# In-place closing operations, half-width tiles at the end, and a second output queue, in a gated mix of local attention and a token MLP

## The chip, the cores and the metric

The kernel runs on one core of one Trainium2 chip. The core has five engines with a queue each: TensorE multiplies matrices into PSUM (eight banks, each of 512 fp32 values in each of 128 partitions), VectorE and ScalarE do elementwise work, GpSimd does little here, and SyncE (SP) issues transfers. Transfers are issued from SP's or ScalarE's queue and run on 16 DMA engines. Engines wait for each other through semaphores. The metric is the device time of one execution in microseconds (us), lower is better.

## What is computed

The output is a mix of two branches with a gate for each of 2048 positions:

```python
# x: [1, 2048, 512] bf16; 32 heads of 16; a window of 8 positions, each 2 apart
g = sigmoid((A_x * gate_w).sum(-1, keepdims=True))
a = local_attention(A_x @ A_wqkv) @ A_wo      # softmax over the window's 8 logits
h = layernorm(B_x)                            # over the 512 columns
u = gelu(einsum("bsd,sf->bdf", h, B_w1) + B_b1)     # mixes positions, F = 1792
b = (einsum("bdf,fs->bds", u, B_w2) + B_b2) transposed back to [1, 2048, 512]
out = g * a + (1 - g) * b
```

The kernel takes `A_x` for both branches, since the reference passes the same array to both (`x = A_x`).

## The kernel before, in words

The 2048 positions are cut into 16 tiles of 128 (`NST = 16`). The program runs in five stages that overlap across engines.

1. **Projections** (lines 626 to 670): Q, K and V come out transposed, columns in partitions, in groups of four matmuls (L631). The first groups are cut into 384 and 128 columns, so that matmuls of three widths occur.
2. **Attention weights** (674 to 781): VectorE multiplies Q and shifted K (L678), TensorE sums over a head's 16 columns (L686), VectorE and ScalarE make the softmax. Thirty-two transfers from ScalarE's queue spread the weights over partitions (L780, recorded as L436, the helper that makes every plain transfer).
3. **Weighted values** (783 to 795): VectorE multiplies V by the weights (L789) and adds the eight window positions, partly in place (L792), into `OT`, the attention's output before its last projection.
4. **MLP** (797 to 904): `ph2` multiplies the normalised x by B_w1 (L804), gelu follows on ScalarE, then `ph3` multiplies by B_w2 (L844), one accumulation of 14 matmuls for each of the 16 output tiles. ScalarE takes each tile out of PSUM with L898: T1[i] = (1 - g) * (y + b2), in bf16. `T1` lies where `X` was.
5. **Closing** (849 to 877, `emit_wo`): for each tile i, four matmuls of 512 columns (`wo_i`, L861) project OT with wo into one of the four PSUM banks 4 to 7, `WB(i)` = 4 + i mod 4. VectorE's closing operation (`cmb_i`, L873) computes g * PSUM + T1[i] and writes it into one of the four buffers `OUTS[i % 4]`. A transfer of 128 KB (`d_out_i`) takes that buffer to the output by SP's queue.

What waits for what is declared by names that an operation reads and writes: `cmb_i` reads the bank and `t1_i` and writes `outs(i % 4)`, which `d_out_i` reads. So `cmb_(i+4)` waits until `d_out_i` has landed, and `wo_(i+4)` until `cmb_i` has read its bank.

The order on each engine comes from a list planner (`_Sched.schedule`, 124 to 232). It repeatedly takes the operation that can start first by the planned durations, and breaks ties by the planned time that is left to the end behind it. Hand-written chains (923 to 937) fix VectorE's whole order, most of ScalarE's and a piece of TensorE's: `ph3b_14`, `wo_0` to `wo_3`, `ph3a_15`, `ph3b_15`, `wo_4`. So wo_4 to wo_15 are the last work on TensorE. At the end SP waits for the four semaphores of the output transfers (L981 to 984), and the program ends.

Of the kernel before, what the change touches and what calls it, by code (L numbers as in the profile page):

```python
# [5 lines left out]
BF16 = mybir.dt.bfloat16  # L6
FP32 = mybir.dt.float32
U8 = mybir.dt.uint8
ALU = mybir.AluOpType
# [4 lines left out]
D = 512  # L14
# [4 lines left out]
NST = S // 128  # L19
# [7 lines left out]
BURST_DELAY = 0.05  # L27
OUTQ = "sp"
XS = 384


class _Op:
# [302 lines left out]
def bass_gated_mix__sliding_local_dilated__mixer_token_mlp__prompt_kernel(nc, A_x, A_wqkv, A_wo, B_x, B_w1, B_b1, B_w2, B_b2, gate_w, out, dbg=None):  # L335
    with contextlib.ExitStack() as es:
        block = es.enter_context(nc.Block())
        view, pview, off, total = _views(nc, es)
        ps = es.enter_context(nc.psum_tensor("ps", [128, 8, 512], FP32))
        esem = {e: es.enter_context(nc.semaphore("sem_" + e)) for e in ("pool", "act", "dve", "pe")}  # L340
        sch = _Sched()
# [6 lines left out]
        outv = out[0].rearrange("(t p) d -> p t d", p=128)  # L348
# [13 lines left out]
        WO = view("WO", BF16, [(D, 4), (1, D)])  # L362
# [4 lines left out]
        OT = view("PBUF", BF16, [(S, 4), (1, S)])  # L367
        ATX = view("ATX", BF16, [(NW * HC, 8), (HC, NW), (1, HC)])
        ATT = view("ATT", BF16, [(NW * HC, 2), (HC, NW), (1, HC)])
        T1 = view("X", BF16, [(D, NST), (1, D)])  # L370
        OUTS = view("OUTS", BF16, [(D, 4), (1, D)])
        IDENT = view("IDENT", BF16, [(1, 128)])
        ONES = view("ONES", BF16, [(1, 128)])
        RP = view("RP", BF16, [(1, 32)])
# [23 lines left out]
        G = small(NST)  # L398
# [9 lines left out]
        def col(v_, i):  # L408
            return bass.AP(v_.tensor, v_.offset + i, [list(v_.ap[0]), [1, 1]])
# [11 lines left out]
        A = sch.add  # L421
# [13 lines left out]
        def mk_dma(dst, src):  # L435
            return lambda e: e.dma_start(dst, src)  # L436
# [42 lines left out]
        wq01 = ld_w(0, 0, 2, "act")  # L479
        ld_xt0(0, XS)  # L480
        xt0b = ld_xt0(XS, 512)
        wq23 = ld_w(0, 2, 2, "act")
# [16 lines left out]
        def ld_w1(j):  # L499
# [4 lines left out]
            if j < 4:  # L504
# [8 lines left out]
                       writes=["wo"], deps=throttle(), after=prev_dma(), name="d_wo")  # L513
# [4 lines left out]
        for i_, (v_, n_) in enumerate(((B_b1, NFT), (B_b2, NST), (gate_w, 4))):  # L518
            vr = v_.rearrange("(t q j) -> q t j", q=4, j=32)
            for q_ in range(4):  # L520
                sch.dma("sp", mk_dma(psub(BR, 32 * q_, n_, 32 * i_, [(1, 32)]), vr[q_]), n_ * 64, ds_b, reads=["br"],
                        writes=["br_%d_%d" % (i_, q_)], deps=throttle(), after=prev_dma(), name="d_b_%d_%d" % (i_, q_), issue=0.45)
        d_w1.append(ld_w1(3))
        A("dve", lambda e: e.transpose(out=BT, in_=BR), 0.2, reads=["br_%d_%d" % (i_, q_) for i_ in range(3) for q_ in range(4)],
          writes=["gwc"], name="t_b")
# [29 lines left out]
        for hf in range(2):  # L555
            t0 = 8 * hf
            for t in range(t0, t0 + 8):
                A("dve", (lambda t_: (lambda e: e.bn_stats(out=ST6[:, t_, :], in_=X[:, t_, :])))(t), 0.59,  # L558
                  reads=["x%d" % t], writes=["st6_%d" % t], name="ln1_%d" % t, prio=0)
# [7 lines left out]
                                                                    in1=cols(ZC, t0_, 8), op0=ALU.mult, op1=ALU.mult)))(t0),  # L567
# [5 lines left out]
              reads=["zc%d" % hf], writes=["sd%d" % hf], name="ln_sqrt%d" % hf, prio=0)  # L573
            A("dve", (lambda t0_: (lambda e: e.reciprocal(out=cols(RSTD, t0_, 8), in_=cols(SD, t0_, 8))))(t0), 0.25,
              reads=["sd%d" % hf], writes=["rstd%d" % hf], name="ln_rstd%d" % hf, prio=0)
            A("dve", (lambda t0_: (lambda e: e.scalar_tensor_tensor(
                out=cols(NMR, t0_, 8), in0=mv(t0_, 0), scalar=-0.5, in1=cols(RSTD, t0_, 8),
                op0=ALU.mult, op1=ALU.mult)))(t0),
# [68 lines left out]
        for (b0, d0, d1, s0, s1) in ((0, 0, 2, 0, XS), (0, 0, 2, XS, 512), (0, 2, 4, 0, 512), (4, 0, 4, 0, 512)):  # L647
            for b in range(b0, b0 + 4):
                tn, dl = first[b]
                last_main[0] = A("pe", f_proj(tn, dl, 0, b, d0, d1, s0, s1), 0.216 * (d1 - d0) * (s1 - s0) / 512,  # L650
                                 reads=ALLXT[s0 // 128:s1 // 128] + ["wqkv%d_%d" % (tn, dt) for dt in range(d0, d1)],
                                 writes=fbn[b], after=[last_main[0]], name="pf_%s%d_%d_%d" % (tnames[tn], dl, d0, s0))
        for b, (tn, dl) in enumerate(first):
            A("act", f_evq(tn, dl, 0, b), 0.52, reads=fbn[b] + (["k5pad"] if tn == 1 else []),
              writes=["%s5_%d_0" % (tnames[tn], dl)], name="ev_%s%d_0" % (tnames[tn], dl), prio=0)
# [7 lines left out]
        for (tn, dl, sb) in seq_proj:  # L663
            xr = ALLXT[4 * sb:4 * sb + 4]
            bank = main_bank()
            last_main[0] = A("pe", f_proj(tn, dl, sb, bank), 0.866,
                             reads=xr + ["wqkv%d_%d" % (tn, dt) for dt in range(4)],
                             writes=["acc%d" % bank], after=[last_main[0]], name="pj_%s%d_%d" % (tnames[tn], dl, sb), prio=0)
            A("act", f_evq(tn, dl, sb, bank), 0.62, reads=["acc%d" % bank] + (["k5pad"] if tn == 1 else ["v5pad"] if tn == 2 else []),
              writes=["%s5_%d_%d" % (tnames[tn], dl, sb)], name="ev_%s%d_%d" % (tnames[tn], dl, sb), prio=0)  # L670
# [26 lines left out]
        for wh in range(2):  # L697
# [6 lines left out]
            for (dl, c0, nc_) in pieces:  # L704
# [3 lines left out]
                  reads=["q5_%d_%d" % (dl, sb) for sb in range(c0, c0 + nc_)] +  # L708
                        ["k5_%d_%d" % (dl, sb) for sb in range(max(c0 - 1, 0), c0 + nc_)] + ["k5pad"],
                  writes=wr, name="qkm_%d_%d_%d" % (wh, dl, c0), prio=0)  # L710
                if c0 + nc_ == 4 and dl % 2 == 1:
# [4 lines left out]
                    else:  # L716
                        for wl in range(4):
                            qop = A("pe", f_qkr(prs, (wl,)), 0.5, reads=rd, writes=["lg%d_0" % (4 + wl), "lg%d_1" % (4 + wl)],
                                    name="qkr_%d_%d_%d" % (wh, dl, wl), prio=-100 + wl, delay=BURST_DELAY)
                            A("act", (lambda wh_, wl_: (lambda e: e.activation(out=ATT[:, :, 4 * wh_ + wl_, :], in_=ps[:, 4 + wl_, :].rearrange("p (h c) -> p h c", h=2), func=AF.Copy)))(wh, wl),  # L720
                              0.55, reads=["lg%d_0" % (4 + wl), "lg%d_1" % (4 + wl)], writes=["lw%d" % (4 * wh + wl)],
                              name="lev_%d_%d" % (wh, wl), prio=0)
# [18 lines left out]
        for hf in range(2):  # L741
            on = ["outs%d" % (2 * hf), "outs%d" % (2 * hf + 1)]
# [4 lines left out]
        for hf in range(2):  # L747
# [3 lines left out]
              reads=["outs1"], writes=["lh%d" % hf] + (wall if hf == 0 else []), name="sm_sub%d" % hf, prio=0)  # L751
            if hf == 0:
                A("act", lambda e: e.activation(out=col(SD, 0), in_=col(ZC, 0), func=AF.Exp, scale=0.0), 1.5,
                  reads=["zc0"], writes=["sd0"], name="sm_pre")
            A("act", (lambda hf_, l_: (lambda e: e.activation(out=ATT[:, hf_], in_=l_, func=AF.Exp)))(hf, lgh), 1.95,  # L755
              reads=["lh%d" % hf], writes=["att%d" % hf], name="sm_exp%d" % hf, prio=0)
        for hf in range(2):
# [5 lines left out]
            def f_rcp(e, hf_=hf):  # L763
# [6 lines left out]
              reads=["rs%d" % hf], writes=["att%d" % hf], name="sm_nrm%d" % hf, prio=0)  # L770
# [4 lines left out]
        for u in range(8):  # L775
            c, hf = u // 2, u % 2
            ds_at = sch.dsem("atx%d" % u)
            for a_ in range(4):
                dst = bass.AP(ATX.tensor, ATX.offset + a_ * pst + u * NW * HC, [[4 * pst, 32], [1, NW * HC]])
                sch.dma("act", mk_dma(dst, psub(ATT, 32 * c, 32, hf * NW * HC, [(1, NW * HC)])), 32 * NW * HC * 2, ds_at, issue=0.62,  # L780
                        reads=["att%d" % hf], writes=["atx_%d_%d" % (u, a_)], deps=pb_readers, name="d_atx_%d_%d" % (u, a_))
        USEQ = [0, 2, 1, 3, 4, 6, 5, 7]
        for k_, u in enumerate(USEQ):
            b_ = HC * u
            pv = PV[k_ % 2]
            pn = "pv%d" % (k_ % 2)
            in0 = sub(V5, PAD + b_, [(-2, NW), (KROW, 4), (1, HC)])
            in1 = sub(ATX, u * NW * HC, [(HC, NW), (0, 4), (1, HC)])
            A("dve", (lambda o_, i0, i1: (lambda e: e.tensor_tensor(out=o_, in0=i0, in1=i1, op=ALU.mult)))(pv, in0, in1), 4.4,  # L789
              reads=v_res + ["atx_%d_%d" % (u, a_) for a_ in range(4)], writes=[pn] + [qk_res, k_all][k_ % 2], name="avm_%d" % u)  # L790
            for (nm, n_, du) in (("ava", 4, 2.25), ("avb", 2, 1.2)):
                A("dve", (lambda pv_, n__: (lambda e: e.tensor_tensor(out=pv_[:, 0:n__], in0=pv_[:, 0:n__], in1=pv_[:, n__:2 * n__], op=ALU.add)))(pv, n_),  # L792
                  du, writes=[pn], name="%s_%d" % (nm, u))
# [15 lines left out]
        for ft in range(NFT):  # L809
            j = ft // 2  # L810
            bank = main_bank()
            for qt in range(4):
                last_main[0] = A("pe", f_ph2(ft, bank, qt), 0.864, reads=["x%d" % t for t in range(4 * qt, 4 * qt + 4)] + ["w1s%d" % (j % 4)],
                                 writes=["acc%d" % bank], after=[last_main[0]], name="ph2_%d_%d" % (ft, qt), prio=0)
            A("act", (lambda ft_, bank_: (lambda e: e.activation(out=UT[:, ft_, :], in_=ps[:, bank_, :], func=AF.Gelu_apprx_tanh,  # L815
                                                                bias=col(B1C, ft_))))(ft, bank), 0.72,
              reads=["acc%d" % bank, "b1c"], writes=["ut%d" % ft] + ALLXT,
              name="gel_%d" % ft, prio=0)
# [32 lines left out]
        def WB(i):  # L851
            return WOB[i % len(WOB)]

        def WBN(i):
            return ["lg%d_0" % WB(i), "lg%d_1" % WB(i)]

        def f_wo(i):
            def fn(e):
                ins = None
                for t in range(4):  # L860
                    ins = e.matmul(ps[:, WB(i), :], lhsT=OT[:, t, 128 * i:128 * i + 128], rhs=WO[:, t, :],  # L861
                                   start=(t == 0), stop=(t == 3))
                return ins
            return fn

        ds_out = [sch.dsem("out%d" % k) for k in range(4)]
        LAG = 4
        pending_wo = []

        def emit_wo(i):  # L870
            A("pe", f_wo(i), 0.866, reads=["ot%d" % (i // 2), "wo"], writes=WBN(i),
              name="wo_%d" % i, prio=0)
            A("dve", (lambda i_: (lambda e: e.scalar_tensor_tensor(out=OUTS[:, i_ % 4, :], in0=ps[:, WB(i_), :], scalar=col(G, i_),  # L873
                                                                   in1=T1[:, i_, :], op0=ALU.mult, op1=ALU.add)))(i), 0.75,
              reads=WBN(i) + ["g", "t1_%d" % i], writes=["outs%d" % (i % 4)], name="cmb_%d" % i, prio=0)
            sch.dma(OUTQ, mk_dma(outv[:, i, :], OUTS[:, i % 4, :]), 128 * D * 2, ds_out[i % 4], issue=(1.0 if OUTQ == "pool" else 0.5),
                    reads=["outs%d" % (i % 4)], name="d_out%d" % i)

        p3bank = {}

# [8 lines left out]
        for i in range(NST):  # L889
# [4 lines left out]
            elif i > 1:  # L894
                emit_ph3(i, 0)
            emit_ph3(i, 1)
            bank = p3bank[i]
            A("act", (lambda i_, bank_: (lambda e: e.activation(out=T1[:, i_, :], in_=ps[:, bank_, :], func=AF.Identity,  # L898
                                                               scale=col(OMG, i_), bias=col(C2, i_))))(i, bank), 0.8,
              reads=["acc%d" % bank, "omg", "c2"], writes=["t1_%d" % i, "x%d" % i],  # L900
              name="t1_%d" % i, prio=0)
# [18 lines left out]
        def lnr(hf):  # L920
# [5 lines left out]
              + ["ln3_%d" % t for t in range(NST) if t not in ln3_act] + ["qkm_1_2_0", "msk_0", "sm_ma0", "sm_mb0", "qkm_1_3_0",  # L926
                 "msk_1", "sm_ma1", "sm_mb1", "sm_m1", "sm_sub0", "sm_sub1", "g_omg", "g_c2", "g_g"]
              + ["%s%d" % (n_, h_) for h_ in range(2) for n_ in ("sm_sa", "sm_sb", "sm_s1", "sm_rcp", "sm_nrm")]
              + ["%s_%d" % (n_, u) for k_ in range(4) for n_ in ("avm", "ava", "avb", "avc") for u in USEQ[2 * k_:2 * k_ + 2]] + ["cmb_%d" % i for i in range(NST)])
        byname["d_w1_6"].deps.add(byname["d_atx_2_3"])  # L930
        chain(["d_w2_0", "d_th0", "d_w2_1", "d_th1", "d_w1_4", "d_w2_2", "d_w1_5", "d_w1_6"])
        def atn(u):
# [25 lines left out]
        def emit_engine(eng_name, e):  # L958
            for op in sch.order[eng_name]:
                for d in op.waits:  # L960
                    if d.is_dma:
                        e.wait_ge(d.dsem.handle, 16 * d.seq)
                    else:
                        e.wait_ge(esem[d.eng], d.seq)
                r = op.fn(e)
                if dbg is not None:
                    rr = r[-1] if isinstance(r, list) else r
                    dbg.setdefault("opmap", []).append((eng_name, op.name, rr.ins.name, op.start, op.end))
                if op.is_dma:
                    r.then_inc(op.dsem.handle, 16)  # L970
                elif op.sig:
                    if isinstance(r, list):
                        r = r[-1]
                    r.then_inc(esem[eng_name], 1)
            if eng_name == "sp" and dbg is not None and "keep" in dbg:
                for d in sch.dsems:
                    n_ = len([o for o in sch.ops if o.is_dma and o.dsem is d])
                    if n_ and d.queue == "sp":
                        e.wait_ge(d.handle, 16 * n_)
            if eng_name == OUTQ:  # L980
                for d in ds_out:  # L981
                    n_ = len([o for o in sch.ops if o.is_dma and o.dsem is d])
                    if n_:
                        e.wait_ge(d.handle, 16 * n_)

        @block.sync
        def _(e):
            emit_engine("sp", e)
# [44 lines left out]
```

## Time and profile before

| what | us |
|---|---|
| median of 3 runs (lowest to highest) | 171.76 (171.66 to 172.13) |
| the profiled execution's own time | 170.96 |
| span of that execution, first to last instruction | 169.2 |
| TensorE busy in the span (850 matmuls) | 163.5 |
| VectorE busy (122 instructions) | 142.8 |
| ScalarE busy (112 instructions) | 74.4 |
| closing operations, L873, 16 of 128 x 512 | 11.7 in all, mean 749 ns |
| output projection, L861, 62 recorded matmuls of 512 columns | 14.0 in all, mean 379 ns |
| output transfers, 16 of 128 KB, SP's queue | 1.7 median from issue to landing |
| mean granted TensorE clock | 0.998 of full speed |

A row "L861 PE MATMUL" is a group of instructions of that source line on that engine. "Busy" is the sum of their durations. Matmuls are pipelined: one is 379 ns long, and the next starts before it has ended, so the distance between starts tells what one costs in a stream. A number in square brackets is the idle time of the engine ahead of an instruction, with what ended it. "SPq" and "ACTq" are the queues in which SyncE and ScalarE issue transfers.

### The profile page before, as it was taken

The page shows a single profiled execution, that of the slowest core. Times are in us where ns is not written, and L with a number is a line of the kernel's source. Part 1 is how long each engine was busy: PE and PEld are TensorE (multiplying, and loading weights), DVE is VectorE, ACT ScalarE, POOL GpSimd, SP SyncE. Part 2 cuts the span into 40 slices and gives each one's busy share as a digit, 9 for nine tenths or more (in the row PEclk, how much of TensorE's full clock was granted, in tenths as well). Part 3 has the DMA queues.
Part 4 walks back from the last instruction along what each step waited for, and adds up shares of the span by engine and source line. Part 5 has one row for each costly group of instructions (what it writes and reads, how often), then busy time and mean ns, then how long its engine had stood idle before and what let it go on. Part 6 is the DMA issues. An engine that isn't in the chain of part 4 may idle for free.

```text
span 169.2 us, 2130 instructions
## 1 busy us (share of the span) xinstructions
PE 163.5 (97%) x850; PEld 76.5 (45%) x865; DVE 142.8 (84%) x122; ACT 74.4 (44%) x112; POOL 1.0 (1%) x9
## 2 busy tenths in 40 slices
PE   7999999999999999999999999999999999999992
PEld 2555555544444444444444444444444444444440
DVE  1009999999999963899999999999999999952874
ACT  0476698898979718691222131131221312211000
POOL 2000000000000000000000000000000000000000
PEclk9999999999999999999999999999999999999999
DMA  5999999939000989973789606472573470002234
GB/s 137 282 299 244 278 326 282 288 105 251 1 0 12 257 175 239 286 188 86 196 222 316 161 16 144 108 200 71 162 217 107 114 217 0 0 27 97 93 128 155
DMA packets 47313, 27.43 MB, mean 162 GB/s; under 512 B 11844, under 2 KB 46148, under 8 KB 47304
## 3 DMA queue, kind: packets, MB, share of 16 engines
q1 hardware_dynamic: 44696, 22.05, 48.6%
q10 hardware_dynamic: 2608, 5.25, 11.9%
q8 instruction: 7, 0.11, 0.3%
q14 instruction: 2, 0.02, 0.0%
HBM read 18.89 MB, written 2.11 MB: 124 GB/s over the span
## 4 chain that ended last, share of the span: by engine, by line
PE 93%; DMA 3%; ACT 2%; issue 1%; DVE 0%
PE ps L844 28%; PE ps L804 28%; PE ps L631 24%; PE ps L861 8%; PE ps L686 3%; DMA arena<-in_A_x_dram 3%; ACT arena L582 1%; DVE arena L873 0%; ACT arena L642 0%
## 5 line engine op out<-in xcount | busy, mean ns | idle before, releaser
L844 PE MATMUL ps<-arena 128*128 128x512 bf16 x220 | 48.5, 379 | 0.2
L804 PE MATMUL ps<-arena 128*128 128x512 bf16 x219 | 48.1, 379 | 0.5 <-ACT arena L582 0.2
L631 PE MATMUL ps<-arena 128*128 128x512 bf16 (+2 forms) x196 | 41.4, 370 | 0.7 <-issue 0.3
L678 DVE TENSOR_TENSOR arena<-arena 128x4096 bf16<-128x4096 bf16 (+1 forms) x12 | 35.6, 2991 | 0.0
L789 DVE TENSOR_TENSOR arena<-arena 128x8192 bf16<-128x8192 bf16 x8 | 35.0, 4419 | 0.0
L804 PEld LDWEIGHTS ps<-arena 128*128 128x128 bf16 x224 | 21.7, 98 | 26.8 <-issue 0.8
L844 PEld LDWEIGHTS ps<-arena 128*128 128x128 bf16 x224 | 21.9, 98 | 26.4
L631 PEld LDWEIGHTS ps<-arena 128*128 128x128 bf16 x200 | 21.9, 113 | 20.5 <-issue 1.0
L898 ACT ACTIVATE arena<-ps,arena 128x512 bf16<-128x512 f32 x16 | 12.5, 778 | 39.4 <-PE ps L844 35.6
L792 DVE TENSOR_TENSOR arena<-arena 128x4096 bf16<-128x4096 bf16 (+1 forms) x16 | 27.0, 1751 | 0.0
L642 ACT ACTIVATE arena<-ps 128x512 bf16<-128x512 f32 x32 | 18.9, 596 | 5.4 <-PE ps L631 5.2
L815 ACT ACTIVATE arena<-ps,arena 128x512 bf16<-128x512 f32 x14 | 9.6, 688 | 24.9 <-PE ps L804 24.7
L558 DVE BATCH_NORM_STATS2 arena<-arena 128x6 f32<-128x512 bf16 x16 | 10.1, 680 | 10.8 <-DMA arena<-in_A_x_dram 10.8
L873 DVE SCALAR_TENSOR_TENSOR arena<-ps,arena 128x512 bf16<-128x512 f32 x16 | 11.7, 749 | 6.7 <-PE ps L861 4.8
L861 PE MATMUL ps<-arena 128*128 128x512 bf16 x62 | 14.0, 379 | 0.1
L639 ACT ACTIVATE arena<-ps 128x512 bf16<-128x512 f32 x16 | 9.0, 596 | 3.8 <-PE ps L631 3.8
L861 PEld LDWEIGHTS ps<-arena 128*128 128x128 bf16 x64 | 6.3, 98 | 7.5
L582 ACT ACTIVATE arena<-arena 128x512 bf16<-128x512 bf16 x12 | 9.2, 803 | 0.0
L736 DVE TENSOR_TENSOR arena<-arena 128x512 bf16<-128x512 bf16 (+4 forms) x11 | 7.3, 667 | 0.8 <-ACT arena L755 0.5
L686 PE MATMUL ps<-arena 128*32 128x512 bf16 x128 | 7.6, 380 | 0.0
L794 DVE TENSOR_TENSOR arena<-arena 128x1024 bf16<-128x1024 bf16 x8 | 5.5, 688 | 0.1
L720 ACT ACTIVATE arena<-ps 128x512 bf16<-128x512 f32 x8 | 4.1, 603 | 2.5 <-PE ps L686 2.5
(42 smaller groups left out, 37.3 us busy)
## 6 DMA issues: line engine op xcount, KB each, us to landing
arena<-in_B_w_dram SPq DMA_DIRECT2D x7, 1024.0 KB, 7.9
arena<-in_B_w_dram SPq DMA_DIRECT2D x8, 896.0 KB, 5.2
arena<-arena ACTq DMA_DIRECT2D x32, 128.0 KB, 2.7
arena<-in_A_x_dram SPq DMA_DIRECT2D x4, 512.0 KB, 5.1
out_dram<-arena SPq DMA_DIRECT2D x16, 128.0 KB, 1.7
arena<-in_A_wqkv_dram ACTq DMA_DIRECT2D x2, 256.0 KB, 2.9
arena<-in_A_wqkv_dram ACTq DMA_DIRECT2D x1, 512.0 KB, 4.3
arena<-in_A_wqkv_dram SPq DMA_DIRECT2D x1, 512.0 KB, 7.1
```

Source lines behind the costliest of these rows:

```text
L582: A("act", (lambda t_: (lambda e: e.activation(out=X[:, t_, :], in_=X[:, t_, :], func=AF.Identity, scale=col(RSTD, t_), bias=col(NMR, t_)) ...
L631: ins = e.matmul(ps[:, bank, s0:s1], lhsT=lhsT, rhs=XT[:, dt, sb * 512 + s0:sb * 512 + s1], start=(dt == 0 and s0 == 0), stop=(dt == 3))
L642: return lambda e: e.activation(out=dst, in_=ps[:, bank, :], func=AF.Copy)
L678: return lambda e: e.tensor_tensor(out=PBL[buf][:, :, 512 * c0:512 * (c0 + nc_)], in0=in0, in1=in1, op=ALU.mult)
L686: ins = e.matmul(ps[32 * c:32 * c + 32, 4 + wl, :], lhsT=RP, rhs=PBL[buf][:, wl, c * 512:(c + 1) * 512], start=(dl == 0), stop=(dl == 3), ...
L789: A("dve", (lambda o_, i0, i1: (lambda e: e.tensor_tensor(out=o_, in0=i0, in1=i1, op=ALU.mult)))(pv, in0, in1), 4.4, reads=v_res + ["atx_% ...
L792: A("dve", (lambda pv_, n__: (lambda e: e.tensor_tensor(out=pv_[:, 0:n__], in0=pv_[:, 0:n__], in1=pv_[:, n__:2 * n__], op=ALU.add)))(pv, n ...
L804: ins = e.matmul(ps[:, bank, :], lhsT=W1W[:, slot, st, 128 * e_:128 * e_ + 128], rhs=X[:, st, :], start=(st == 0), stop=(st == NST - 1))
L844: ins = e.matmul(ps[:, bank, :], lhsT=W2S[slot][:, ft, 128 * e_:128 * e_ + 128], rhs=UT[:, ft, :], start=(ft == 0), stop=(ft == NFT - 1))
L861: ins = e.matmul(ps[:, WB(i), :], lhsT=OT[:, t, 128 * i:128 * i + 128], rhs=WO[:, t, :], start=(t == 0), stop=(t == 3))
L873: A("dve", (lambda i_: (lambda e: e.scalar_tensor_tensor(out=OUTS[:, i_ % 4, :], in0=ps[:, WB(i_), :], scalar=col(G, i_), in1=T1[:, i_, :] ...
L898: A("act", (lambda i_, bank_: (lambda e: e.activation(out=T1[:, i_, :], in_=ps[:, bank_, :], func=AF.Identity, scale=col(OMG, i_), bias=co ...
```

## The change

Three things change, all in the closing stage, and two lines follow from them.

- `cmb_i` writes its result over T1[i], and the output transfer reads T1[i]. The `OUTS` view is no longer used for output (the region stays for other uses).
- From tile 12 on (`HT0 = 12`) a tile is projected in two halves of 256 columns: four matmuls of 256 columns into one bank, a closing operation of 256 columns, then the same for the second half in the next bank. The halves count on in the rotation of the four banks.
- Tiles 12 to 14 still leave in one transfer, after both halves. Tile 15 leaves in two of 64 KB: the first half by SP's queue, the second by ScalarE's, each as soon as its half is done.
- VectorE's hand-written order names the halves, and SP waits at the end for the added semaphore too.

```diff
+HT0 = 12
...
-        OUTS = view("OUTS", BF16, [(D, 4), (1, D)])
...
-        def f_wo(i):
+        def f_wo(i, bank, c0=0, c1=D):
             def fn(e):
                 ins = None
                 for t in range(4):
-                    ins = e.matmul(ps[:, WB(i), :], lhsT=OT[:, t, 128 * i:128 * i + 128], rhs=WO[:, t, :],
+                    ins = e.matmul(ps[:, bank, 0:c1 - c0], lhsT=OT[:, t, 128 * i:128 * i + 128], rhs=WO[:, t, c0:c1],
                                    start=(t == 0), stop=(t == 3))
                 return ins
             return fn
...
+        ds_outb = sch.dsem("outb")
...
         def emit_wo(i):
-            A("pe", f_wo(i), 0.866, reads=["ot%d" % (i // 2), "wo"], writes=WBN(i),
-              name="wo_%d" % i, prio=0)
-            A("dve", (lambda i_: (lambda e: e.scalar_tensor_tensor(out=OUTS[:, i_ % 4, :], in0=ps[:, WB(i_), :], scalar=col(G, i_),
-                                                                   in1=T1[:, i_, :], op0=ALU.mult, op1=ALU.add)))(i), 0.75,
-              reads=WBN(i) + ["g", "t1_%d" % i], writes=["outs%d" % (i % 4)], name="cmb_%d" % i, prio=0)
-            sch.dma(OUTQ, mk_dma(outv[:, i, :], OUTS[:, i % 4, :]), 128 * D * 2, ds_out[i % 4], issue=(1.0 if OUTQ == "pool" else 0.5),
-                    reads=["outs%d" % (i % 4)], name="d_out%d" % i)
+            parts = [(0, D)] if i < HT0 else [(0, D // 2), (D // 2, D)]
+            ons = []
+            for h, (c0, c1) in enumerate(parts):
+                k_ = i if len(parts) == 1 else HT0 + 2 * (i - HT0) + h
+                bank, bn = WB(k_), WBN(k_)
+                sfx = "" if len(parts) == 1 else "ab"[h]
+                frac = (c1 - c0) / D
+                on = "o%d%s" % (i, sfx)
+                ons.append(on)
+                A("pe", f_wo(i, bank, c0, c1), 0.866 * frac, reads=["ot%d" % (i // 2), "wo"], writes=bn, name="wo_%d%s" % (i, sfx), prio=0)
+                A("dve", (lambda i_, b_, c0_, c1_: (lambda e: e.scalar_tensor_tensor(
+                    out=T1[:, i_, c0_:c1_], in0=ps[:, b_, 0:c1_ - c0_], scalar=col(G, i_), in1=T1[:, i_, c0_:c1_],
+                    op0=ALU.mult, op1=ALU.add)))(i, bank, c0, c1), 0.08 + 0.67 * frac, reads=bn + ["g", "t1_%d" % i], writes=[on],
+                  name="cmb_%d%s" % (i, sfx), prio=0)
+                if i == NST - 1:
+                    q = "act" if sfx == "b" else "sp"
+                    sch.dma(q, mk_dma(outv[:, i, c0:c1], T1[:, i, c0:c1]), 128 * (c1 - c0) * 2,
+                            ds_out[i % 4] if q == "sp" else ds_outb, issue=0.5, reads=[on], name="d_out%d%s" % (i, sfx))
+            if i < NST - 1:
+                sch.dma("sp", mk_dma(outv[:, i, :], T1[:, i, :]), 128 * D * 2, ds_out[i % 4], issue=0.5, reads=ons, name="d_out%d" % i)
...
-                for d in ds_out:
+                for d in ds_out + [ds_outb]:
```

More of the change, by code (lines that the diff above doesn't have):

```diff
@@ L928, in bass_gated_mix__sliding_local_dilated__mixer_token_mlp__prompt_kernel @@
               + ["%s%d" % (n_, h_) for h_ in range(2) for n_ in ("sm_sa", "sm_sb", "sm_s1", "sm_rcp", "sm_nrm")]
-              + ["%s_%d" % (n_, u) for k_ in range(4) for n_ in ("avm", "ava", "avb", "avc") for u in USEQ[2 * k_:2 * k_ + 2]] + ["cmb_%d" % i for i in range(NST)])
+              + ["%s_%d" % (n_, u) for k_ in range(4) for n_ in ("avm", "ava", "avb", "avc") for u in USEQ[2 * k_:2 * k_ + 2]] + ["cmb_%d" % i for i in range(HT0)] + ["cmb_%d%s" % (i, x_) for i in range(HT0, NST) for x_ in "ab"])
         byname["d_w1_6"].deps.add(byname["d_atx_2_3"])
```

## The prediction, made before the changed kernel had run

> **What bounds the kernel now.** I read the page's chain of waits first, then the same chain in order of time for the last 15 us, then single instructions of that stretch, and last the rows that price what the change adds.
>
> ```profile
> ## 4 chain that ended last, share of the span: by engine, by line
> PE 93%; DMA 3%; ACT 2%; issue 1%; DVE 0%
> ...
> 155.87 6.47 PE ps L861 x30
> 162.35 0.05 issue
> 162.40 3.85 PE ps L861 x17
> 166.25 0.02 issue
> 166.27 0.75 DVE arena L873
> ```
>
> TensorE sets the end until 166.25 us. From 155.87 it does nothing but the output projection (L861), twelve tiles in 10.38 us, 0.865 us each. Behind its last matmul stands a serial tail: one closing operation of 0.75 us on VectorE (L873), one transfer out, the end of the program at 169.2. A change that touches only tiles 12 to 15 and the closing operations can gain in that tail of 2.95 us, or lose by making TensorE's stream longer or by holding up VectorE.
>
> ```profile
> 156.78 1.61 DVE L873 SCALAR_TENSOR_TENSOR arena<-ps,arena 128x512 bf16<-128x512 f32 x2 [3.13 <-PE ps L861]
> ...
> 161.96 0.75 DVE L873 SCALAR_TENSOR_TENSOR arena<-ps,arena 128x512 bf16<-128x512 f32 x1
> 163.62 1.41 DVE L873 SCALAR_TENSOR_TENSOR arena<-ps,arena 128x512 bf16<-128x512 f32 x2 [0.91 <-DMA out_dram<-arena]
> ...
> 165.60 1.42 DVE L873 SCALAR_TENSOR_TENSOR arena<-ps,arena 128x512 bf16<-128x512 f32 x2
> ...
> 167.05 0.33 SPq L436 DMA_DIRECT2D out_dram<-arena  x1
> ...
> 100.67 0.48 ACTq L436 DMA_DIRECT2D arena<-arena  x1
> ```
>
> The second column is the stretch from the first start to the last end. Two closing operations that wait for TensorE take 1.61, so they start 0.86 apart; two that have work waiting take 1.41, so VectorE can start one every 0.66. The closing operation of tile 11 stands behind a transfer: it started at 163.62 where 161.96 + 0.866 = 162.83 was due, 0.79 late. Each later tile wins back 0.866 - 0.66 = 0.21, four tiles 0.83. So the last one is on time at 166.27, but only by 0.01 (165.60 + 0.66 = 166.26): the whole reserve was used.
>
> ```profile
> L736 DVE TENSOR_TENSOR arena<-arena 128x512 f32<-128x512 f32 x2 | 1.4, 692 | 0.1
> L736 DVE TENSOR_TENSOR arena<-arena 128x256 f32<-128x256 f32 x2 | 0.8, 424 | 0.1
> ...
> 5.91 0.65 PE L631 MATMUL ps<-arena 128*128 128x384 bf16 x3
> 6.72 0.39 PE L631 MATMUL ps<-arena 128*128 128x128 bf16 x4
> ...
> DMA  0000499999964000026899997530000000000000
> ...
> DMA  0000000000000000000000059995504399246799
> ...
> DMA packets 272, 0.14 MB, mean 348 GB/s; under 512 B 0, under 2 KB 272, under 8 KB 272
> ...
> q8 instruction: 1, 0.02, 2.9%
> ```
>
> The last four lines are stretches of the DMA view. The digits are the busy tenths in forty slices of 0.05 us: from 167.0, where the last two output transfers leave, and from 100.6, where the ACT queue starts from empty. Below them stand 113.0 to 113.4, where only the 512-byte rows of the second MLP weight move, and 160.9 to 163.6, where an instruction fetch sits among the output transfers.
>
> **Part 1, in place.** The closing operation reads and writes T1 where it wrote one of four OUTS buffers. It costs nothing in itself: L792 in place takes 2284 ns for 4096 elements, L678 with another output 2282. What goes is each wait for an output transfer, among them the 0.91. On this execution that is worth 0: what hides it is TensorE, for the last closing operation starts right behind its last matmul with or without the wait. Nothing overwrites T1 afterwards, so no new wait comes in its place.
>
> **Part 2, TensorE.** Sixteen matmuls of 512 columns become 32 of 256, each with its own weight load. A 512-column one starts every (3.85 - 0.379)/16 = 0.217 us; three of 384 take 0.65 with 0.326 for one, so 0.162 apart; four of 128 take 0.39 with 0.219 for one, so 0.057. That is straight in the columns, with weight loads of 113 ns hidden even at 0.057. Halfway between the two, 256 columns cost 0.1095: 32 x 0.1095 = 3.50 for 16 x 0.217 = 3.47, **+0.03** (bounds 0 and +0.10, the latter if each load showed by 2 ns).
>
> Against this stands a rule of the Trainium skill, "TensorE: Matmul & The Clock Gate", section Back-to-back issue gap: in a real stream of weight loads and matmuls the spacing at 128 columns was 81 ns, not the 56 of the bare formula. This trace has 57 at that size, but over eight matmuls only. If 25 ns came on each of the 32, the term would be +0.8 and the sum +0.6.
>
> A half also waits for its PSUM bank, last used four halves before. A half takes TensorE 0.437. The tightest is the second half of tile 13 on tile 11's bank: it starts 3 x 0.437 = 1.31 after tile 11's last matmul, and tile 11's closing operation is done 0.04 + 0.75 = 0.79 after it, 0.52 to spare. Between halves it is 1.31 against 0.52. Nothing stalls while VectorE keeps pace.
>
> **Part 3, VectorE.** Eight closing operations of 256 columns for four of 512. The f32 pair says what 256 elements fewer save: 692 - 424 = 268 ns. So 750 - 268 = 482 ns, and a pace of 0.66 - 0.27 = 0.39, under TensorE's 0.437: VectorE does not fall behind. In the tail the last one is shorter, **-0.27** (bounds -0.29 by the ratio 424/692, and -0.25). The other seven lie under TensorE; without that cover each costs 0.39.
>
> **Part 4, the last tile's transfers.** Before, the issue at 167.05 on SP was followed by packets from the 18th slice, about 167.87 (0.82), to the 27th, about 168.40; from there to 169.2 runs completion and the end. Now the first half goes by SP some 0.44 before the second, its packets gone before the second's begin, and the second by the ACT queue, empty since the attention weights; only the end of the program is queued behind it. What an ACT issue of a 128 x 512-byte store costs, no row shows. The ACT row lasts 0.48 where SP's lasts 0.33, and its first packet came in the 24th slice, about 1.12 after its start: +0.30 over SP, for 32 rows of 4 KB between SBUF tiles. If all of that belongs to that shape, 0. I take **+0.20**, nearer to the row of the queue in question. The packets: 128 as before, of 512 bytes. 128 KB took 0.53; at the 348 GB/s of the 512-byte rows 64 KB take 0.19 and 128 KB 0.38, so **-0.15** for the part that grows with bytes (bounds 0 if a packet costs the same, -0.25 if all halves). SP waits for one semaphore more at the end: **+0.02** (0 to 0.07).
>
> The skill's "DMA: Bandwidth & Descriptors", Rules for kernel authors, says of two transfers to partition halves that they are not worth it, since both run on the same 16 engines. These are halves by columns, one 0.44 us before the other. Should they queue all the same, the -0.15 goes, and the sum is -0.02.
>
> **The sum.** +0.03 - 0.27 + 0.20 - 0.15 + 0.02 = -0.17 us; by the ends, -0.54 to +0.22. The profiled execution took 170.96 for its span of 169.2; the runs' median is 171.76, 0.80 above. I subtract from that: **171.59**, with an own range of 171.2 to 172.0. About 0.3% (0.52 us) is what a measurement of this kernel can tell from no change, so most of this forecast lies within it.
>
> **Rival A: the output wait costs time in ordinary runs.** In the profile the late closing operation was made good with 0.01 to spare. If the transfer of tile 7, which shared an engine with the fetch (2.9% of 16 x 2.7 us = 1.25 us on one engine), lands any later in the runs that were timed, their end moves by as much, and in-place writing takes all of it away. For it: a fetch belongs to a place in TensorE's stream, so it comes in every run; the timed runs are 0.70 to 1.17 longer than the profiled one. Against: no view shows where those 0.80 lie. Half of them: 171.59 - 0.40 = 171.2; all: 170.8.
>
> **Rival B: VectorE becomes the bound of the last four tiles, slower.** If two halves don't overlap as full ones do and the pace isn't 0.39, the delay grows by seven times its excess over 0.437. From a pace of 0.437 + 0.17/7 = 0.46 on the kernel is slower than before, from 0.437 + 0.69/7 = 0.54 by more than 0.3%. At 0.50 (482 and a wake-up): +0.44 - 0.17, 172.0. At the full tile's 0.66 with its 750 ns: 1.56 + 0.27 - 0.17, 173.4. At 0.56: 172.3. Against it: the two f32 rows.
>
> **Rival C: the order elsewhere moves.** The planner ranks everything by the planned time left to the end, and that changes: eight times 0.415 planned on VectorE for four times 0.75, same plan on TensorE. An early tie could break otherwise, and the change would then not be only in the tail. Against: VectorE's order and most of ScalarE's are written out by hand. Either sign, some 0.7: 170.9 or 172.3.
>
> **How the numbers follow.** Forecast 0.52, A 0.26, B 0.14, C 0.08. Faster by over 0.3%: most of A (0.22), the forecast's low end (0.05), half of C (0.04): 0.31. Slower: B from 0.54 on (0.10), half of C (0.04), the forecast's unknowns (0.02): 0.16. Within: 0.53. The range is 170.95 to 172.15: it leaves out the far end of A and B's high paces.
>
> **What would show it.** On the changed profile: matmuls of 256 columns 0.109 apart; halves of 0.48 on VectorE, starting 0.44 apart and never idle for a transfer; the last one ending 0.24 earlier than before, at 166.78 if nothing ahead has moved; an ACT issue right behind it, with packets 0.8 to 1.1 later. Wrong it is if VectorE's halves come at over 0.46, if matmuls are further apart, if the clock or the order before 150 us differs, or if the timed gain is above the change in the profiled tail (that is A).

## The result, and the profile after

Over 22 runs of each, the changed kernel takes 171.03 us (median) against 171.63 before: a ratio of 0.9972 with a 95% interval of 0.9961 to 0.9984, so 0.48 us faster (0.27 to 0.67); the two medians differ by 0.60. The forecast was 171.59 in a range of 170.95 to 172.15, a gain of 0.17 from a median of three runs, 171.76. The time lies near the low end of the range. The direction is right and the size too small: 0.17 lies below the interval of the gain. The profiled execution took 170.60 for a span of 168.9, against 170.96 and 169.2.

The chain of the changed kernel, share of the span on the page and then in order of time (start, length, what), and its closing operations by shape (busy time, mean ns, idle time before them with what ended it):

```profile
PE 95%; DMA 3%; DVE 1%; issue 0%
...
155.87 9.98 PE ps L861 x60
165.84 0.02 issue
165.87 0.92 DVE arena L882 x2
```

```profile
L861 PE MATMUL ps<-arena 128*128 128x256 bf16 x32 | 3.7, 272 | 0.0
L882 DVE SCALAR_TENSOR_TENSOR arena<-ps,arena 128x512 bf16<-128x512 f32 x12 | 9.0, 751 | 6.0 <-PE ps L861 4.9
L882 DVE SCALAR_TENSOR_TENSOR arena<-ps,arena 128x256 bf16<-128x256 f32 x8 | 3.3, 478 | 0.0
```

The closing operation has moved from L873 to L882 in the source. TensorE still sets the end, up to the last two halves on VectorE, and no idle time in front of a closing operation is ended by an output transfer any more. Single instructions of the last stretch:

```profile
162.83 0.60 PE L861 MATMUL ps<-arena 128*128 128x256 bf16 x4
...
165.87 0.92 DVE L882 SCALAR_TENSOR_TENSOR arena<-ps,arena 128x256 bf16<-128x256 f32 x2
...
166.82 0.37 ACTq L436 DMA_DIRECT2D out_dram<-arena  x1
```

Four matmuls of 256 columns take 0.60 with 0.272 for one: 0.109 apart. Two halves on VectorE take 0.92 with 0.48 for one: 0.44 apart, TensorE's pace. The last transfer is issued at 166.82, where before it was 167.05. Its packets, in forty slices of 0.05 us from 167.0:

```profile
DMA  9995347996410158996300000000000000000000
```

The last block is the second half, by ScalarE's queue: it begins in the 14th slice, at 167.66, 0.84 after the issue, and ends in the 21st, at 168.03. It takes 0.37 where the whole tile took 0.53.

To compare kernels I use one length from each trace, the **tail**: from the first matmul of the closing stage (L861) to the end of the span. It is 149.236 to 169.216 before, 19.98, and 149.228 to 168.870 after, 19.64. It leaves out what differs between executions without having to do with the closing stage: over the fourteen profiles of all kernels here, the first projection matmul starts anywhere from 5.41 to 5.80, and from there to the closing stage takes 143.81 to 144.48. In four profiles of the kernel before alone it is 5.42 to 5.73 and 143.81 to 144.00.

### The profile page after: what moved, and what is told of

Same layout as the page of the kernel before. It is cut to its first block, busy times and chain, and to the rows that moved or that the text cites. A ratio compares the mean times of both kernels' runs of the same rounds, so it can differ in the third digit from the quotient of the medians.

```text
span 168.9 us, 2174 instructions
## 1 busy us (share of the span) xinstructions
PE 164.3 (97%) x881; PEld 78.0 (46%) x881; DVE 143.3 (85%) x126; ACT 74.4 (44%) x112; POOL 1.0 (1%) x9
## 3 DMA queue, kind: packets, MB, share of 16 engines
q10 hardware_dynamic: 2752, 5.31, 11.9%
## 4 chain that ended last, share of the span: by engine, by line
PE 95%; DMA 3%; DVE 1%; issue 0%
PE ps L804 29%; PE ps L844 29%; PE ps L631 25%; PE ps L861 8%; PE ps L686 4%; DMA arena<-in_A_x_dram 3%; PE ps L606 1%; DVE arena L882 1%
## 5 line engine op out<-in xcount | busy, mean ns | idle before, releaser
L804 PE MATMUL ps<-arena 128*128 128x512 bf16 x224 | 48.7, 379 | 0.0
L844 PE MATMUL ps<-arena 128*128 128x512 bf16 x224 | 48.7, 379 | 0.0
L631 PE MATMUL ps<-arena 128*128 128x512 bf16 (+2 forms) x200 | 42.0, 371 | 0.7 <-DMA arena<-in_A_x_dram 0.7
L804 PEld LDWEIGHTS ps<-arena 128*128 128x128 bf16 x224 | 21.7, 98 | 26.8 <-issue 0.8
L844 PEld LDWEIGHTS ps<-arena 128*128 128x128 bf16 x224 | 21.9, 98 | 26.4
L631 PEld LDWEIGHTS ps<-arena 128*128 128x128 bf16 x200 | 21.9, 113 | 20.7 <-issue 1.2
L882 DVE SCALAR_TENSOR_TENSOR arena<-ps,arena 128x512 bf16<-128x512 f32 (+1 forms) x20 | 12.2, 642 | 6.0 <-PE ps L861 4.9
L861 PE MATMUL ps<-arena 128*128 128x512 bf16 (+1 forms) x80 | 14.2, 336 | 0.0
L861 PEld LDWEIGHTS ps<-arena 128*128 128x128 bf16 x80 | 7.8, 98 | 6.2
```

The costliest lines, as they stand in the source:

```text
L631: ins = e.matmul(ps[:, bank, s0:s1], lhsT=lhsT, rhs=XT[:, dt, sb * 512 + s0:sb * 512 + s1], start=(dt == 0 and s0 == 0), stop=(dt == 3))
L804: ins = e.matmul(ps[:, bank, :], lhsT=W1W[:, slot, st, 128 * e_:128 * e_ + 128], rhs=X[:, st, :], start=(st == 0), stop=(st == NST - 1))
L844: ins = e.matmul(ps[:, bank, :], lhsT=W2S[slot][:, ft, 128 * e_:128 * e_ + 128], rhs=UT[:, ft, :], start=(ft == 0), stop=(ft == NFT - 1))
L861: ins = e.matmul(ps[:, bank, 0:c1 - c0], lhsT=OT[:, t, 128 * i:128 * i + 128], rhs=WO[:, t, c0:c1], start=(t == 0), stop=(t == 3))
L882: A("dve", (lambda i_, b_, c0_, c1_: (lambda e: e.scalar_tensor_tensor(out=T1[:, i_, c0_:c1_], in0=ps[:, b_, 0:c1_ - c0_], scalar=col(G, i ...
```

## The experiments

All ratios are against the kernel before, run beside them; each tail is that of one profile. "Late" is the delay of tile 11's closing operation against one tile every 0.863.

| kernel | ratio, 95% interval | tail, us | late, us |
|---|---|---|---|
| before (profile shown above) | | 19.98 | 0.80 |
| before, second profile | | 20.33 | 1.16 |
| before, third | | 20.38 | 1.21 |
| before, fourth | | 19.99 | 0 (tile 12: 0.26) |
| changed kernel | 0.9972 (0.9961 to 0.9984) | 19.64 | 0 |
| in place alone | 0.9987 (0.9969 to 1.0005) | 19.99 | 0 |
| halves and two queues, OUTS kept | 1.002 (0.9995 to 1.0045) | 20.82 | 1.24 |
| changed, both halves by SP | 0.9969 (0.9952 to 0.9985) | 19.68 | 0 |
| changed, only tile 15 halved | 0.9984 (0.9967 to 1.0002) | 19.79 | 0 |
| changed, tile 15 in one transfer | 0.9962 (0.9944 to 0.998) | 19.76 | 0 |
| in place, full tiles, last transfer split | 0.9986 (0.9968 to 1.0005) | 20.08 | 0 |
| before, three buffers | 1.008 (1.005 to 1.011) | 21.80 | 1.99 |
| before, fetch moved earlier | 0.998 (0.9961 to 0.9998) | 19.99 | tile 9: 0.99 |
| changed, last tile in thirds | 0.997 (0.9951 to 0.999) | 19.69 | 0 |

The intervals are 0.4 to 1.0 us wide, so runs alone tell only the larger effects apart; the terms of 0.1 are read from the traces, where matmul paces repeat within 0.01.

**In place alone.**

```diff
-out=OUTS[:, i_ % 4, :]   ...   writes=["outs%d" % (i % 4)]
+out=T1[:, i_, :]         ...   writes=["o%d" % i]
-mk_dma(outv[:, i, :], OUTS[:, i % 4, :])
+mk_dma(outv[:, i, :], T1[:, i, :])
```

> In place alone, full tiles, one transfer each. Tail theory (all of the gain is the shorter tail): no gain, 0.0 us against the kernel before, between -0.1 and +0.1; in the trace VectorE never idles for an output transfer and the last closing operation still starts 0.04 us behind the last matmul. Wait theory (rival A: the output wait costs time in ordinary runs): -0.1 to -0.4 us from this edit alone.

The tail is 19.99, as in the profile of before: nothing gained against that execution. VectorE waits for TensorE alone, as its only row of waits from 150 to 167.7 us shows (total, times, longest):

```profile
DVE arena L873 <- PE ps L861: 4.9, 2, 3.1
```

The runs lie 0.22 below before, from 0.53 below to 0.09 above, which fits both theories. They had to be told apart otherwise.

**The kernel before again.** Three more profiles of the same program.

> The kernel before once more, for a second profile of its output wait. Wait theory (the landing of tile 7's transfer varies from run to run, and beyond 0.8 us of lateness of tile 11's closing operation the end moves with it): a lateness other than 0.79 by some tenths; if it is x above 0.8, 19.98 + x from the closing stage's first matmul to the end of the span. If the wait is the same in every run: 0.79 again, and 19.98.

> The kernel before a third time, for one more profile of the output wait. Wait theory: a lateness L of tile 11's closing operation anywhere from 0.7 to 1.3, and 19.98 + max(0, L - 0.80) from the closing stage's first matmul to the end of the span, within 0.03. If the first repeat was an accident: 0.8 and 19.98.

> The kernel before a fourth time, as the third: the end moves one for one with the lateness above 0.80, and not below it.

Closing operations of the second, third and fourth profile, from the first that follows tile 3's to the last:

```profile
156.94 5.93 DVE L873 SCALAR_TENSOR_TENSOR arena<-ps,arena 128x512 bf16<-128x512 f32 x7 [3.13 <-PE ps L861]
164.15 3.38 DVE L873 SCALAR_TENSOR_TENSOR arena<-ps,arena 128x512 bf16<-128x512 f32 x5 [1.28 <-DMA out_dram<-arena]
```

```profile
157.12 5.93 DVE L873 SCALAR_TENSOR_TENSOR arena<-ps,arena 128x512 bf16<-128x512 f32 x7 [3.14 <-PE ps L861]
164.38 3.38 DVE L873 SCALAR_TENSOR_TENSOR arena<-ps,arena 128x512 bf16<-128x512 f32 x5 [1.33 <-DMA out_dram<-arena]
```

```profile
157.17 6.79 DVE L873 SCALAR_TENSOR_TENSOR arena<-ps,arena 128x512 bf16<-128x512 f32 x8 [3.13 <-PE ps L861]
164.33 3.08 DVE L873 SCALAR_TENSOR_TENSOR arena<-ps,arena 128x512 bf16<-128x512 f32 x4 [0.37 <-DMA out_dram<-arena]
```

In the first profile five closing operations behind the wait took 3.41 and the last one waited for TensorE again. Here they take 3.38, all at VectorE's own pace of 0.66: VectorE was still behind at the end. Lateness 1.16 and 1.21 gives tails of 20.33 and 20.38, that is 19.98 + 0.36 and + 0.41 expected. In the fourth the wait fell on tile 12, 0.26 late, which three tiles win back, and the tail is 19.99. There the fetch began 12.2 after the stage's first matmul, in the other three 11.9, so that it held up tile 8's transfer and no longer tile 7's. The chain of the second profile runs through the transfer:

```profile
156.04 6.00 PE ps L861 x28
162.04 2.68 DMA out_dram<-arena
...
164.81 0.33 DVE arena L873
```

So the wait is worth 0, 0.35, 0.40 and 0 in four executions, 0.19 in the mean. In-place writing takes that away: in the profile of in place alone, tile 7's transfer landed 3.7 after its issue, as late as in the second profile of before, and the tail stayed at 19.99 where the rule above gives 20.34. The same rule tells, as an estimate, what the late landings of the other in-place profiles would have cost with the buffers: 0.25 in the changed kernel's own, at most 0.07 in the other five. With those seven the mean over eleven executions is 0.13: the 0.19 is no more exact than that.

**The fetch moved.** If the instruction fetch causes the late landing, moving it in TensorE's stream must move the late tile.

```diff
                     ins = e.matmul(ps[:, 7, :], lhsT=WARM[:, 0:128], rhs=WARM, start=True, stop=True)
+                for _ in range(8):
+                    ins = e.matmul(ps[:, 7, 0:16], lhsT=WARM[:, 0:128], rhs=WARM[:, 0:16], start=True, stop=True)
                 return ins
```

> The kernel before with eight more matmuls of 16 columns in TensorE's warm-up (they compute nothing that is used), so that everything after them stands 16 instructions later in TensorE's stream and the instruction fetch of the closing stage comes two tiles sooner, near 159.4 after a projection start at 5.4. Fetch theory: the transfer of tile 5 is hit in place of tile 7's, tile 9's closing operation is late by 0.8 to 1.2, six tiles win back up to 1.28, and the tail is 19.98 whatever the lateness: 0.1 to 0.3 us faster than the kernel before, less if the longer warm-up delays the start. If the lateness has nothing to do with the fetch: tile 11 is late as before.

Closing operations (now L875), then the DMA view of 159.0 to 161.7 in slices of 0.0675 us:

```profile
156.76 4.20 DVE L875 SCALAR_TENSOR_TENSOR arena<-ps,arena 128x512 bf16<-128x512 f32 x5 [3.13 <-PE ps L863]
162.07 4.94 DVE L875 SCALAR_TENSOR_TENSOR arena<-ps,arena 128x512 bf16<-128x512 f32 x7 [1.10 <-DMA out_dram<-arena]
```

```profile
DMA  0002989985100000289997410101010010000025
...
q8 instruction: 1, 0.02, 3.4%
```

The wait now stands in front of tile 9: five operations run ahead of it instead of seven. The single packet of the instruction queue takes 3.4% of 16 engines over 2.7 us, 1.47 us on one engine; the scattered 1s after the second block fit that engine's packets of the two transfers it held up, while the other fifteen were done (the profile does not name engines). The fetch began 10.05 after the stage's first matmul, against 11.8 to 12.3 in every other profile. Tile 9 is 0.99 late, tile 10 0.79, tile 11 0.59, and the tail is 19.99 although the lateness is above 0.80. Both parts of the theory hold: the fetch sets which tile waits, and the tiles that remain set how much is won back. The time falls by 0.34 (0.03 to 0.67) with no change in the closing stage's code.

**Three buffers.** `OUTS[:, i_ % 3, :]` for `% 4` in the kernel before.

> The kernel before with three OUTS buffers in place of four, so each closing operation waits for the transfer three tiles back. Reserve theory (the kernel before absorbs its output wait with 0.01 us to spare): the transfer of tile 7 now holds tile 10's closing operation until about 163.6, 1.5 late, VectorE wins back 0.21 for each of five tiles, and the last one starts about 166.9 instead of 166.27: +0.5 to +0.7 us. If the wait had room to grow instead: 0.0, within 0.1.

```profile
157.73 5.08 DVE L873 SCALAR_TENSOR_TENSOR arena<-ps,arena 128x512 bf16<-128x512 f32 x6 [3.09 <-PE ps L861]
165.10 2.07 DVE L873 SCALAR_TENSOR_TENSOR arena<-ps,arena 128x512 bf16<-128x512 f32 x3 [2.29 <-DMA out_dram<-arena]
167.71 2.07 DVE L873 SCALAR_TENSOR_TENSOR arena<-ps,arena 128x512 bf16<-128x512 f32 x3 [0.53 <-DMA out_dram<-arena]
```

No room to grow, as the reserve theory says, but more than it says: 0.8% (0.5% to 1.1%), a tail of 21.80. The first wait was larger than in my sum: tile 7's transfer landed 3.9 after its issue, and tile 10 is 2.2 late where I had 1.5. And my sum had one wait: the late operation issues its own transfer late, and with three buffers that one holds up tile 13 a second time (0.53).

**Halves without in place.** The changed kernel, with the OUTS buffers kept and each half waiting for the transfer four tiles back.

```diff
-out=T1[:, i_, c0_:c1_]   ...
+out=OUTS[:, i_ % 4, c0_:c1_]   ...   deps=[douts[i - 4]] if h else [],
```

> The changed kernel with the four OUTS buffers kept: halves and two queues, but not in place, so the waits for output transfers return. Independent parts (the in-place edit is worth nothing by itself, so nothing without it either): -0.35 us against the kernel before, as the changed kernel. Enabler theory: tile 11's closing operation starts near 163.6 again, and with halves VectorE wins back only 0.437 - 0.39 = 0.04 per half, so the last half starts 163.62 + 0.66 + 7 x 0.392 = 167.02 instead of 166.31, 0.7 later than in the changed kernel: +0.3 to +0.5 us against the kernel before.

```profile
157.15 5.93 DVE L884 SCALAR_TENSOR_TENSOR arena<-ps,arena 128x512 bf16<-128x512 f32 x7 [3.13 <-PE ps L862]
164.44 3.88 DVE L884 SCALAR_TENSOR_TENSOR arena<-ps,arena 128x512 bf16<-128x512 f32 x9 [1.36 <-DMA out_dram<-arena]
...
PE ps L862 <- DVE arena L884: 0.8, 1, 0.8
```

The first two rows are VectorE's instructions, the last is TensorE's waits. With halves VectorE wins back almost nothing, and TensorE itself now waits 0.8 for a bank, because four halves back is two tiles back. The tail is 20.82, 0.65 above the mean of before's four, and 0.44 above the third of them, which was nearly as late (1.21). In the runs it is 0.2% slower (from 0.05% faster to 0.45% slower), which alone does not tell it from before; its interval lies above that of the changed kernel. The two parts of the change are not independent: without in-place writing the gain is gone, and in this profile the halving loses.

**Where the halving of tiles 12 to 14 comes in.** `HT0 = 15` for 12.

> The changed kernel with only tile 15 in halves (HT0 = 15). If the halving of tiles 12 to 14 does nothing: the changed kernel's time, in the trace 19.64 us from the first projection matmul of the closing stage to the end of the span (before: 19.98). Runway theory (a full closing operation occupies VectorE for 0.66, a half comes from TensorE after 0.437, so the first half starts 0.22 late and each later one wins back 0.045; only six or seven halves make that good): the last half starts 0.18 late, 19.82 in the trace, 0.18 slower than the changed kernel.

The chain of this kernel at its end:

```profile
166.26 0.04 DVE arena L882
166.30 0.63 issue
166.93 0.48 DVE arena L882
```

The first half of tile 15 starts one full operation's 0.66 behind tile 14's, and the chain stays on VectorE from there. The tail is 19.79 (19.82 expected, 0.15 above the changed kernel). In the changed kernel the halves after the first win that back, with one to spare: the seventh and the eighth wait for TensorE again.

**The transfers.** Three variants: the last tile whole after both halves; two column halves issued together after a full closing operation (with `HT0 = 16`); both halves by SP. The edits stand in this order, each in part.

```diff
-                if i == NST - 1:
+                if False:
...
-            if i < NST - 1:
+            if True:
...
-                    q = "act" if sfx == "b" else "sp"
...
+                    for q, c0, c1 in (("sp", 0, D // 2), ("act", D // 2, D)):
...
-                    q = "act" if sfx == "b" else "sp"
+                    q = "sp"
```

> The changed kernel with the last tile leaving in one transfer of 128 KB after its second half. Terms of the sum as the trace gives them: matmuls +0.03 and closing operation -0.27 stay, the transfer's -0.12 goes: 19.74 to 19.77 us from the closing stage's first matmul to the end of the span (changed kernel 19.64, before 19.98), some -0.23 us against the kernel before. If the two transfers are worth nothing: 19.64.

> In place, full tiles, and the last tile's two column halves issued at the same moment by SP and ScalarE's queue. Shared engines theory (both run on the same 16 DMA engines, so what counts is that the first half leaves 0.44 earlier): 19.98 us from the closing stage's first matmul to the end of the span, within 0.05, no gain over in place alone. Parallel theory (two queues move 128 KB faster than one): 19.83 to 19.88.

> The changed kernel with both halves of the last tile leaving by SP's queue. Step of the prediction (an ACT issue costs 0.20 more than an SP issue): 0.2 us faster than the changed kernel, first packets 0.82 after the issue. Other theory (an ACT issue of this shape costs what an SP issue costs, 0.84 against 0.82 to the first packet in the changed kernel's trace): same time as the changed kernel within 0.05 in the trace's tail, some -0.35 us against the kernel before.

One transfer: 19.76, so the earlier and shorter second half is worth 0.12. Split but issued together: 20.08, which is 0.09 worse than in place alone, above what either theory allowed and nearer to the first: the packets of the two queues share the engines.

```profile
167.58 0.33 SPq L436 DMA_DIRECT2D out_dram<-arena  x1
167.59 0.37 ACTq L436 DMA_DIRECT2D out_dram<-arena  x1
...
DMA  0499999973000000003699999986300000000000
```

The last block is the two halves, eleven slices of 0.05 with something in them and 0.55 in all, no shorter than the 0.53 of the whole tile. Both by SP: 19.68, and the last half is issued at 166.99 and lands 1.62 later, against 1.57 by ScalarE's queue. The queue makes no difference that matters (0.04 in the tail); a second half that leaves behind the first does.

**Thirds.** Tile 15 in parts of 192, 192 and 128 columns.

> The changed kernel with tile 15 in three parts of 192, 192 and 128 columns, leaving by SP, ScalarE's queue and SP. By the paces measured (VectorE 0.126 + columns/960, TensorE 0.00171 per column): the last part starts 0.11 behind TensorE and takes 0.35 where the half took 0.48: 0.03 gained there, and 0.02 to 0.05 on a transfer of 32 KB: 19.56 to 19.62 from the closing stage's first matmul to the end of the span, against 19.64. If the third transfer's packets of 256 bytes or its issue behind another cost more than that: 19.66 or above.

19.69, worse by 0.05, so the changed kernel stays the fastest tail. The last part took 0.345 as worked out. But the first third starts behind tile 14's second half and not behind TensorE: its operations of 192 columns start 0.32 apart, hardly faster than TensorE's four matmuls (0.33), so almost nothing is won back, and the end of the last operation is 0.04 later. SP also passed two waits in a row after the last landing.

## Why the prediction was right in direction and short in size

**That the time lies in the range is partly luck.** The range of the forecast alone was 171.2 to 172.0, and 171.03 lies below it. It is inside the stated range because that one reached down to 170.95 for rival A. The median of three runs from which I subtracted, 171.76, was also 0.13 above that of 22; from 171.63 the same sum gives 171.46.

**The sum, term by term**, forecast and then measured in the changed trace:

| term | forecast | measured | from |
|---|---|---|---|
| matmuls | +0.03 | +0.04 | last matmul's end, from the stage's start: 17.00, then 17.04 |
| last closing operation | -0.27 | -0.27 | 750 ns, then 482 |
| ScalarE's queue over SP | +0.20 | +0.02 | issue to first packet 0.82, then 0.84 |
| packets | -0.15 | -0.16 | 0.53, then 0.37 |
| end of the program | +0.02 | 0.00 | last landing seen by SP to the span's end: 0.46 both |
| sum | -0.17 | -0.37 | tail 19.98, then 19.64: -0.34 |

The 0.03 between the last two lies mostly in reading packets by slices of 0.05: from the issue to the end of the last packet it is 1.34 and then 1.22 by the packets themselves, so the two rows of the transfer make -0.12 together. For the end of the program I had given no row.

**One term was mis-sized: the issue from ScalarE's queue**, +0.20 forecast, +0.02 measured. I gave the row of the queue (0.48 long, 32 rows of 4 KB) more weight than the row of the shape. The issue took 0.37 here, against 0.33 for SP's 1 KB rows, and 0.37 for the first half that SP issued with the same shape. In these rows what an issue costs followed the transfer, not the queue. The "both halves by SP" run confirms it: 19.68 against 19.64.

**Rival A was true beside the forecast, not instead of it.** The forecast set the wait at 0 because the profile had made it good with 0.01 to spare. Four profiles show that this was one case of several: 0, 0.35, 0.40, 0. With the mean of 0.19 and the tail's 0.34 the gain is 0.53, with 0.13 for the wait 0.47; the runs say 0.48 (0.27 to 0.67). My sign for A, a timed gain above the change in the profiled tail, does not settle it, since 0.34 lies in that interval; the profiles do. What I argued from, the 0.80 by which runs exceeded the profile, is this wait only in part: the spans of the three further profiles exceed the first by 0.52, 0.74 and 0.40, and their tails by 0.35, 0.40 and 0.01. The rest is a later start of the projections and a longer stretch up to the closing stage.

**"VectorE does not fall behind" was right in the outcome and incomplete.** The pace of a half is 0.39 as worked out. But the first half comes 0.437 after a full one that holds VectorE for 0.66, so it starts 0.22 late, and the rest win back 0.045 each: they start 0.39 apart, and only the last two 0.43 to 0.44 behind the one before, as I had forecast for all. Eight halves suffice; with two it costs 0.15.

**Rival B** (a pace above 0.437) fell by the same 0.39. One of its sums was off: at a pace of 0.56 it gives 172.45 and not 172.3. **Rival C** fell too: up to the closing stage each engine issues the same instructions in the same order, as far as they are recorded (some matmul records are missing; the 788 weight loads agree).

Over 32 matmuls of 256 columns the distance is 109 ns, on the line through 57 at 128 columns and 162 at 384. The rule of the Trainium skill, "TensorE: Matmul & The Clock Gate", Back-to-back issue gap, 81 ns at 128 columns in a real stream, does not hold here, and the 25 ns that it would add to each matmul did not come. The skill's rule in "DMA: Bandwidth & Descriptors", Rules for kernel authors, that two transfers to partition halves are not worth it, carried over to these column halves, held where both left together (+0.09) and not where the first left 0.44 ahead (-0.12).

## What to carry to other kernels

Where a serial tail follows the last matmul, halve the last operation, but begin the halving early enough: a full operation just ahead of the first half costs its excess over TensorE's pace, and that has to be won back before the end. A buffer wait that the profile shows as absorbed is free only in that execution; compare its reserve with how much the awaited transfer varies, and profile the same kernel several times. As far as the few rows here go, price an issue by the shape of its transfer first and by its queue second.

## What the runs showed of the hardware that was not expected

An instruction fetch of 16 KB is one packet on one DMA engine. In the closing stage it took 0.88 to 1.68 us in the fourteen profiles, and a transfer spread over 16 engines lands only when that one has done its share behind it: in the first profile the fetch ended at 162.33, single packets went on until 163.03, and the transfer landed at 163.52, 3.38 us after its issue, against 1.7 in the median. Its place follows TensorE's stream: 16 instructions more ahead of it brought it forward by 1.8 to 2.2 us, and the late tile moved by two.
